# Attention scores of batches 1 to 3: one fp32 product, or two float32r products from a wider stack

## The chip, the cores and the metric

The kernel runs on one core of one Trainium2 chip. A core has a matmul engine (TensorE, PE in the rows; its weight loads are listed apart as PEld), a vector engine (VectorE, DVE), a scalar engine (ScalarE, ACT), a third elementwise engine (GpSimd, POOL) and a queue that issues the DMAs (SyncE, SP). Each engine works through its own list of instructions in order and waits for the others by semaphores. The metric is the time of one execution on the device, in microseconds (us), lower is better.

## The reference

Three stages follow one another: causal attention with a decay, and two feed-forward layers without a skip. Cut to what matters:

```python
# q, k, v: [4 batches, 8 heads, 576 tokens, 64], f: [4, 8, 576], all fp32
scores = 0.125 * q @ k^T + cum[:, None] - cum[None, :]     # cum = cumsum(log(clip(f)))
attn = softmax(causal(scores)) @ v                          # [4, 8, 576, 64] -> x: [2304, 512]
h = x @ w_in                                                # [512, 2048]
x = (h * tanh(softplus(h))) @ w_out                         # [2048, 512], weights arrive as float64
h = x @ w2_in
out = (h * cos(h)) @ w2_out                                 # [2304, 512]
```

The four weight matrices arrive in eight-byte floats and are taken apart on the chip.

## The kernel before

**Numbers in two parts.** TensorE takes fp32 operands, or float32r operands, which are fp32 words with fewer bits of the mantissa. The feed-forward products are done in float32r: a matrix is split in a high part (`h` at the end of a name) and the low rest (`l`), and three products (high by high, high by low, low by high) are added up in PSUM. The scores are done in plain fp32, in one product each.

**The stack.** For a pair of heads the attention keeps one tile `stk` with 128 rows. For the query side rows 0 to 63 hold q/8 transposed, rows 64 to 95 hold -1, row 96 holds `cum`, the rest 0. For the key side rows 0 to 63 hold k, row 64 holds `cum`, rows 96 to 127 hold 1. So one product over 128 rows gives the scaled score and the decay together. `prep_job` (L402) fills a stack: DMAs of `cum` (L410, L411), PE transposes of q and k (L429), and copies from PSUM into the stack, three of four on ACT (L445), one on DVE (L447). There are two stacks in turn (`ring`).

**Jobs and items.** A job is a pair of heads of one batch. In batch 0 a pair is cut in two jobs, (8 jobs, numbers 0 to 7); batches 1 to 3 give 12 more (8 to 19). A job of batches 1 to 3 has five items, blocks of queries, which see 64, 192, 320, 448 and 576 keys. For each item and head: `scores` (L453) issues the product (`product`, L461), DVE adds the mask and takes the maximum (L506), ACT takes the exponential (L512), POOL multiplies by the reciprocal of the sum (L526), PE transposes (L563), and PE multiplies by v (L588). An item of 576 keys is cut in two, 384 and 192 keys, since a bank of PSUM holds 512 columns.

**The filler.** From the end of the first token block of batch 0 on, PE gets other work between the attention's products: `hidden_units` (L158) computes the first layer's h for tokens that attention has finished. A unit is 12 products of 128 by 128 weights with 256, 288 or 320 tokens (`in_products`, L153); there are 128 units, and a credit spreads them over the steps of the attention. They go through the token ranges one after another. A unit needs its piece of `w_in` converted; `weight()` has this done at once if it isn't. `split_weights` (L87) does it: a DMA of 512 KB into one of three `raw` buffers, three DVE operations (L123, L124, L133), one on POOL or ACT, one on ACT (L137) and one on POOL (L138).

**The order on each engine** is that of a scheduler that reorders the written program. After the attention the rest of the units run with the conversion of `w_out`, then the two layers to the end.

Of the kernel before, what the change touches and what calls it, by code (L numbers as in the profile page):

```python
# [37 lines left out]
def tile_attention_two_ffn(  # L38
# [12 lines left out]
    nc = tc.nc  # L51
# [18 lines left out]
    rawp = ctx.enter_context(tc.tile_pool(name="raw", bufs=3))  # L70
# [8 lines left out]
    cumd = dram.tile([B * H, S], F32, name="cumd")  # L79
# [7 lines left out]
    def split_weights(layer, nm, pool, early=False):  # L87
# [18 lines left out]
        PF = 2  # L106
# [51 lines left out]
    def hidden_units(tiles, p, hbank, ready):  # L158
        for t0, T in tiles:
            while not ready(t0 + T):  # L160
                yield None
            b, at = divmod(t0, S)
            xh, xl = (xb[b][:, x, :, at : at + T] for x in range(2))
            for j in range(NJ):
                t = hbank()[:, 0:T]
                in_products(t, 1, j, xh, xl)
                if j % 2 == 0:
                    hs = p.tile([128, 2, 320], F32, tag="hs", name="hs")[:, :, 0:T]
                    nc.scalar.activation(out=hs[:, 0], in_=t, func=AF.Copy)  # L169
                else:  # L170
                    marks["v1"] = nc.vector.tensor_copy(hs[:, 1], t)
                    nc.sync.dma_start(out=hd[:, j - 1 : j + 1, t0 : t0 + T], in_=hs)
# [171 lines left out]
    def attention_units(p, bank):  # L344
# [10 lines left out]

        def span(jb):
# [45 lines left out]
        def prep_job(jb):  # L402
# [4 lines left out]
            st = ring[jb % len(ring)]  # L407
            h0 = b * H + 2 * hp
            src = cums[0][h0 : h0 + 2] if jb == 0 else cumd[h0 : h0 + 2]
            nc.sync.dma_start(out=st[96:97, :, 0], in_=src)  # L410
            nc.sync.dma_start(out=st[64:65, :, 1], in_=src)  # L411
            if jb == 0:
                marks["cum"] = nc.sync.dma_start(out=cumd, in_=cums[0])
# [12 lines left out]
            for g in groups:  # L426
# [3 lines left out]
                for which, lo in ((0, qlo), (1, 0)):  # L430
# [4 lines left out]
                    n = len(run)  # L435
                    for j in range(2):
                        i_ = t[64 * j : 64 * j + 64, at : at + n * P]
                        if jb == 0:
                            o = st[0:64, j, which, lo:khi].rearrange("r (p c) -> r c p", c=C)[:, c0 : c0 + n]
                            i_ = i_.rearrange("r (c p) -> r c p", p=P)  # L440
                        else:
                            o = st[0:64, j, which, lo + c0 * P : lo + (c0 + n) * P]
                        sc = 0.125 if which == 0 else 1.0
                        if which or j:
                            nc.scalar.activation(out=o, in_=i_, func=AF.Copy, scale=sc)  # L445
                        else:
                            nc.vector.tensor_scalar(out=o, in0=i_, scalar1=sc, scalar2=None, op0=ALU.mult)  # L447
# [5 lines left out]
        def scores(jb, i):  # L453
            st = ring[jb % len(ring)]
# [6 lines left out]
            def product(o, j, c0, c1, first=QS[i], m=r):  # L461
                at = 2 * j * S + first
# [360 lines left out]
```

## Time and profile before

| | |
|---|---|
| median of 3 runs | 1070.87 us (1069.82 to 1072.17) |
| the profiled execution | 1069.01 us, of which its span is 1067.2 us |
| PE busy | 1035.0 us, 97% of the span, 6112 instructions |
| DVE, ACT, POOL busy | 582.2, 543.3, 199.9 us |
| the score products (L463) | 384 records, 111.6 us busy (records overlap) |

A matmul's own duration in the rows holds its way through the array, so that records overlap; what a product takes from PE in a dense stretch is the distance from its start to the next one's. An fp32 product has two records. The start of a product that follows an fp32 one is shown early (28 ns after the fp32 record's start), so distances are taken to the second product behind it, less what the first takes. Times are counted from the start of the span.

### The profile page before, as it was taken

The numbers are of one execution on the slowest core, as the hardware profiler recorded it, in microseconds if no ns is written. First come the engines' busy times: TensorE is split into PE (matmuls) and PEld (weight loads), VectorE is DVE, ScalarE is ACT, GpSimd is POOL, SyncE is SP. The second block draws the span as 40 slices with busy tenths as digits, with TensorE's granted clock in tenths as the row PEclk, the third lists the DMA queues.
The fourth block names the chain that finished last, engine by engine and source line by source line (L and its number), as shares of the span: only waits on it lengthen the run. The fifth ranks groups of instructions, "written<-read, shape, count | busy, mean of one in ns | idle before, by whom it ended". The sixth has DMA issues, their size and how long they took to land. (4 is left out here: it accounts for less than half of the span.)

```text
span 1067.2 us, 17238 instructions
## 1 busy us (share of the span) xinstructions
PE 1035.0 (97%) x6112; PEld 904.2 (85%) x6112; DVE 582.2 (55%) x1390; ACT 543.3 (51%) x1168; POOL 199.9 (19%) x275
## 2 busy tenths in 40 slices
PE   5898999999999999999999999999999999999998
PEld 4577888888888889978788888899999999999997
DVE  6857544644444435756775257876445454454553
ACT  4766555655555546445656455654434343443433
POOL 6738312222111111422112002110000000000000
PEclk9999999999999999999999999999999999999999
DMA  5756422322231117765968364412010020100000
GB/s 146 179 148 167 135 73 71 91 79 79 80 83 53 57 57 238 224 201 156 326 197 310 113 200 119 143 35 89 1 60 31 1 89 1 60 31 1 30 1 29
DMA packets 119381, 111.55 MB, mean 105 GB/s; under 512 B 66672, under 2 KB 92272, under 8 KB 119296
## 3 DMA queue, kind: packets, MB, share of 16 engines
q1 hardware_dynamic: 119296, 110.46, 34.4%
q8 instruction: 48, 0.79, 0.3%
q14 instruction: 37, 0.30, 0.1%
HBM read 77.32 MB, written 33.10 MB: 103 GB/s over the span
## 5 line engine op out<-in xcount | busy, mean ns | idle before, releaser
L153 PE MATMUL h<-xb,wih 128*128 128x288 f32 (+2 forms) x848 | 190.9, 315 | 0.5 <-ACT hs L169 0.5
L153 PEld LDWEIGHTS h<-xb,wih 128*128 128x128 f32 x848 | 139.1, 190 | 11.5 <-issue 5.9
L153 PE MATMUL h<-xb,wil 128*128 128x288 f32 (+2 forms) x424 | 127.5, 302 | 0.0
L463 PE MATMUL s<-stk 128*128 128x192 f32 (+7 forms) x384 | 111.6, 419 | 9.9 <-DMA stk<-s 4.0
L526 POOL TENSOR_SCALAR s<-s,sm 128x448 f32<-128x448 f32 (+5 forms) x144 | 86.8, 616 | 166.0 <-DVE sm L524 137.2
L246 PE MATMUL acc<-wol,gh 128*128 128x512 f32 x288 | 112.7, 391 | 0.0
L246 PE MATMUL acc<-woh,gh 128*128 128x512 f32 x288 | 112.2, 390 | 0.5 <-DVE stage L268 0.5
L246 PE MATMUL acc<-woh,gl 128*128 128x512 f32 x288 | 112.2, 391 | 0.0
L512 ACT ACTIVATE s<-s,mx 128x448 f32<-128x448 f32 (+5 forms) x144 | 83.5, 581 | 52.6 <-DVE mx L506 47.6
L308 DVE TENSOR_TENSOR gl<-hl,gh 128x512 fp32r<-128x512 f32 x72 | 64.0, 890 | 67.8 <-ACT gh L303 67.7
L153 PE MATMUL hx<-x,wih 128*128 128x384 f32 x384 | 99.6, 336 | 0.0
L153 PE MATMUL h<-x,wih 128*128 128x384 f32 x384 | 97.7, 336 | 0.0
L294 ACT ACTIVATE n<-n 128x384 f32<-128x384 f32 x96 | 50.4, 525 | 91.1 <-DVE n L288 90.4
L308 DVE TENSOR_TENSOR gl<-e,gh 128x384 fp32r<-128x384 f32 x96 | 58.2, 606 | 61.3 <-ACT gh L303 61.2
L506 DVE CUSTOM_DVE_ANT_0 s<-s,maskt 128x384 f32<-128x384 f32 (+6 forms) x152 | 67.7, 453 | 37.3 <-PE s L463 30.1
L463 PEld LDWEIGHTS s<-stk 128*128 128x128 f32 (+1 forms) x384 | 64.7, 199 | 25.5 <-issue 7.1
L153 PEld LDWEIGHTS h<-xb,wil 128*128 128x128 f32 x424 | 80.4, 190 | 0.9 <-issue 0.5
L303 ACT ACTIVATE gh<-e 128x384 fp32r<-128x384 f32 x96 | 50.4, 525 | 58.6 <-DVE e L299 53.5
L138 POOL TENSOR_TENSOR wol<-raw,woh 128x512 fp32r<-128x512 f32 x32 | 44.8, 1399 | 181.3 <-ACT woh L137 176.9
L277 ACT ACTIVATE hl<-hl 128x512 f32<-128x512 f32 x72 | 45.2, 630 | 56.8 <-DMA hl<-hd 47.8
L153 PEld LDWEIGHTS hx<-x,wih 128*128 128x128 f32 x384 | 70.2, 188 | 3.8
L153 PEld LDWEIGHTS h<-x,wih 128*128 128x128 f32 x384 | 70.1, 188 | 3.7
(108 smaller groups left out, 2130.3 us busy)
## 6 DMA issues: line engine op xcount, KB each, us to landing
hl<-hd SPq DMA_DIRECT2D x72, 256.0 KB
raw<-in_moe_w_in_dram SPq DMA_DIRECT2D x32, 512.0 KB
raw<-in_moe_w_out_dram SPq DMA_DIRECT2D x32, 512.0 KB
hd<-hs SPq DMA_DIRECT2D x48, 288.0 KB
x<-yd SPq DMA_DIRECT2D x48, 192.0 KB
yd<-stage SPq DMA_DIRECT2D x32, 256.0 KB
natk<-in_k_dram SPq DMA_DIRECT2D x32, 144.0 KB
out_dram<-stage SPq DMA_DIRECT2D x18, 256.0 KB
```

The source lines that it names most:

```text
L138: nc.gpsimd.tensor_tensor(out=lo[sl], in0=f(high), in1=f(hi[sl]), op=ALU.subtract)
L153: nc.tensor.matmul(o, lhsT=a[wsl], rhs=b[:, kk, :], start=(kk == 0 and i == 0), stop=(kk == NK - 1 and i == 2),)
L246: nc.tensor.matmul(acc[ti][m], lhsT=a[:, ms], rhs=b[:, j % 2, :], start=(start and i == 0), stop=(end and i == 2),)
L277: nc.scalar.activation(out=e, in_=e, func=AF.Mish, scale=UNSCALE)
L294: nc.scalar.activation(out=t, in_=t, func=AF.Sin, scale=TWO_PI)
L303: nc.scalar.activation(out=gh, in_=e, func=AF.Copy)
L308: marks["v1"] = nc.vector.tensor_tensor(out=gl, in0=st.pop(n)[0], in1=f(gst[n][0]), op=ALU.subtract)
L463: marks["score"] = nc.tensor.matmul(o, lhsT=st.rearrange("p j w s -> p (j w s)")[0:128, at : at + m], rhs=st[0:128, j, 1, c0:c1], start=Tr ...
L506: marks["ttr"] = nc.vector.tensor_tensor_reduce(out=s[rows, c0:c1], in0=o, in1=mk, scale=-1.0, scalar=BIG if prev is None or rows.start el ...
L512: nc.scalar.activation(out=s[:, 0:w], in_=s[:, 0:w], func=AF.Exp, scale=-1.0, bias=mx, accum_out=sm[:, j : j + 1])
L526: nc.gpsimd.tensor_scalar(out=s[:, 0:w], in0=s[:, 0:w], scalar1=sm[:, j : j + 1], scalar2=1.0, op0=ALU.mult, op1=ALU.mult)
```

## The change

From batch 1 on the stack has four parts in place of two, in float32r: `[q high; q low]`, `[k high; k high]`, `[q high; -1, cum]` and `[k low; cum, 1]`, where `cum` itself is given as a high and a low row. A score product is then two products into one place of PSUM: (q high + q low) by k high, and q high by k low plus the decay. The high part is written by ACT (rounded to float32r), the low part by DVE (the source less the high part), and the second copies of the high parts by POOL. Batch 0 keeps fp32 stacks, with `cum` in two rows as well. One float32r stack is made at the start, the other takes the place of the fp32 stacks when batch 0's scores are done. The preparation of the next job begins nine half-steps before a job's end, where five were used before. Items of 576 keys are cut at 288. `hidden_units` now takes, two units at a time, a token range for which the next weights are converted, and only otherwise the least advanced one. During the attention there are two `raw` buffers and one load ahead (three and two before); the three come back behind it.

```diff
 prep_job
-            nc.sync.dma_start(out=st[96:97, :, 0], in_=src)
-            nc.sync.dma_start(out=st[64:65, :, 1], in_=src)
+            for row, x in ((96, 0), (64, 1)) if whole(jb) else ((96, 2), (64, 3)):
...
+                    for j in range(2):
+                        i_ = t[64 * j : 64 * j + 64, at : at + n * P]
+                        hi = part(slice(0, 64), which, j)
+                        nc.scalar.activation(out=hi, in_=i_, func=AF.Copy, scale=sc)
+                        nc.vector.scalar_tensor_tensor(
+                            out=part(lo_r, lo_x, j), in0=i_, scalar=sc, in1=f(hi), op0=ALU.mult, op1=ALU.subtract
+                        )
+                    both = slice(0, 2)
+                    dup = (slice(0, 64), 2) if which == 0 else (slice(64, 128), 1)
+                    nc.gpsimd.tensor_copy(part(*dup, both), f(part(slice(0, 64), which, both)))
 scores
+                for x in range(2):
+                    at = (4 * x + j) * S + first
+                    marks["score"] = nc.tensor.matmul(
+                        o, lhsT=st.rearrange("p x j s -> p (x j s)")[0:128, at : at + m],
+                        rhs=st[0:128, 2 * x + 1, j, c0:c1], start=(x == 0), stop=(x == 1),
+                    )
...
-                cuts = [(0, w)] if w <= 512 else [(0, 384), (384, w)]
+                cuts = [(0, w)] if w <= 512 else [(0, w // 2), (w // 2, w)]
 attention_units
+        def new_stack(pool, name, dt, en):
+            one = dt == F32
+            t = pool.tile([128, 2 if one else 4, 2, S], dt, name=name, bufs=1)
+            q, k = (t[:, 0], t[:, 1]) if one else (f(t[:, 2]), f(t[:, 3]))
+            nc.gpsimd.memset(q[96:128], 0.0)
+            nc.gpsimd.memset(k[64:96], 0.0)
+            en.memset(q[64:96], -1.0)
+            en.memset(k[96:128], 1.0)
+            return t
...
+        stack(late - 1)
...
-                begin = max(0, 2 * len(bl) - 5)
+                begin = max(0, 2 * len(bl) - (9 if jb + 1 < len(jobs) and not whole(jb + 1) else 5))
 hidden_units
+            have = [tl for tl in can if (1, todo[tl] // 2, "i") in converted]
+            t0, T = have[0] if have else min(can, key=todo.get)
 split_weights
-        PF = 2
+        PF = 1 if early else 2
 decay_tables
-        cums.append(cum)
+        ch, cl = (x.bitcast(F32R) for x in (ft, one))
+        nc.scalar.activation(out=ch, in_=cum, func=AF.Copy)
+        nc.vector.tensor_tensor(out=cl, in0=cum, in1=ft, op=ALU.subtract)
+        cums.extend((ft, one))
```

In the lists that follow, a row is a line of the kernel, an operation, what it writes and reads, a shape and a count. First PE, at the item of 576 keys of a late job (job 16) of the kernel before; `s` is a bank for the scores, `h` one of the filler's.

```order
L463 MATMUL s_3745<-stk_102 128x448
L463 MATMUL s_3747<-stk_102 128x448
...
L463 MATMUL s_3827<-stk_102 128x384
L463 MATMUL s_3829<-stk_102 128x384
L153 MATMUL h<-xb,wih_339 128x288 x2
L153 MATMUL h<-xb,wil_340 128x288
L153 MATMUL h<-xb,wih_339 128x288
L463 MATMUL s_3831<-stk_102 128x192 x2
```

The same place on PE with the change; `stkr` is a float32r stack, and line numbers are those of the changed kernel.

```order
L509 MATMUL s_4035<-stkr_128 128x448 x2
...
L509 MATMUL s_4038<-stkr_128 128x448 x2
...
L509 MATMUL s_4101<-stkr_128 128x288 x2
L509 MATMUL s_4104<-stkr_128 128x288 x2
L509 MATMUL s_4107<-stkr_128 128x288 x2
L509 MATMUL s_4110<-stkr_128 128x288 x2
L154 MATMUL h<-xb,wih_350 128x288 x2
```

Each fp32 product has become a pair of float32r products, and the item of 576 keys takes four banks (four names `s_`) where it took three, the two heads having shared the bank of the 192-wide part.

Second POOL, at the start of the program before: clearing of the stacks, the masks `maskt` and `mask` and then the first multiplication by a reciprocal.

```order
L607 MEMSET stk_118 32x2x576
L608 MEMSET stk_118 32x2x576
L609 MEMSET stk_118 32x2x576
L610 MEMSET stk_118 32x2x576
L666 AFFINE_SELECT maskt<-maskt 128x128
L672 AFFINE_SELECT mask_68<-mask_68 64x64 x2
L526 TENSOR_SCALAR s<-s,sm 128x128 x2
```

POOL at the same place with the change.

```order
L655 MEMSET stk_123 32x1152
L656 MEMSET stk_123 32x1152
L657 MEMSET stk_123 32x1152
L658 MEMSET stk_123 32x1152
L655 MEMSET stkr_128 32x1152
L656 MEMSET stkr_128 32x1152
L657 MEMSET stkr_128 32x1152
L658 MEMSET stkr_128 32x1152
L732 AFFINE_SELECT maskt<-maskt 128x128
L738 AFFINE_SELECT mask_68<-mask_68 64x64 x2
L572 TENSOR_SCALAR s<-s,sm 128x128 x2
```

Four more memsets, of the first float32r stack, stand ahead of the step that completes `maskt`.

Third PE at the beginning of job 8, the first job of batch 1, before: from its 64-key products to its 320-key products.

```order
L463 MATMUL s_1274<-stk_102 128x64 x2
L153 MATMUL h<-xb,wih_1171 128x256 x2
L153 MATMUL h<-xb,wil_1172 128x256
...
L463 MATMUL s_1347<-stk_102 128x192 x2
L588 MATMUL s_1283<-p,natv 64x128 x2
L153 MATMUL h<-xb,wih_1171 128x256 x4
...
L463 MATMUL s_1421<-stk_102 128x320
L463 MATMUL s_1423<-stk_102 128x320
```

The same stretch with the change.

```order
L509 MATMUL s_1301<-stkr_128 128x64 x4
L634 MATMUL s_1312<-p,natv 64x256 x8
L634 MATMUL s_1312<-p,natv 64x128 x2
L598 MATMUL s_1359<-ident,s 128x128 x3
L509 MATMUL s_1389<-stkr_128 128x192 x4
L634 MATMUL s_1402<-p,natv 64x64 x6
L449 MATMUL s_1411<-ident,natq 128x96 x5
...
L154 MATMUL h<-xb,wih_1202 128x256 x4
```

Filler has left this stretch. Counted over the whole list, 96 products (8 units) of the filler stand between the first 64-key products of jobs 8 and 9 before, and 28 (2.3 units) with the change; at the first 64-key product of job 12 both lists have some 33 units behind them, and at that of job 15 both have 51.

## Rows read from the trace of the kernel before

**Rows 1.** The profile's page: span, and busy time of PE.

```profile
span 1067.2 us, 17238 instructions
PE 1035.0 (97%) x6112; PEld 904.2 (85%) x6112; DVE 582.2 (55%) x1390; ACT 543.3 (51%) x1168; POOL 199.9 (19%) x275
```

**Rows 2.** Stretches: length, busy us of PE, PEld, DVE, ACT, POOL; clock, DMA share, GB/s.

```profile
0.00:47.40 47.40, 31.14 (x161) 21.40 (x161) 34.96 (x106) 29.22 (x81) 32.03 (x54) 0.96 0.63 161
90.00:114.00 24.00, 21.23 (x159) 17.04 (x158) 18.50 (x46) 13.71 (x37) 17.01 (x20) 0.93 0.68 179
140.00:400.00 260.00, 259.12 (x1883) 224.64 (x1882) 114.86 (x461) 136.56 (x366) 53.94 (x111) 1.00 0.26 73
```

**Rows 3.** Timeline of PE, a job of batch 2: start, us, engine, line, operation, count.

```profile
272.79 0.43 PE L153 MATMUL h<-xb,wih 128*128 128x288 f32 x2
...
273.18 1.67 PE L463 MATMUL s<-stk 128*128 128x448 f32 x4
...
274.34 0.78 PE L153 MATMUL h<-xb,wih 128*128 128x288 f32 x2
...
274.96 0.29 PE L153 MATMUL h<-xb,wil 128*128 128x288 f32 x1
```

**Rows 4.** Timeline of PE: fp32 score products of 64 and 192 keys.

```profile
285.27 0.33 PE L463 MATMUL s<-stk 128*128 128x64 f32 x2
285.41 0.51 PE L153 MATMUL h<-xb,wih 128*128 128x288 f32 x2
285.76 0.30 PE L153 MATMUL h<-xb,wil 128*128 128x288 f32 x1
...
287.97 0.82 PE L463 MATMUL s<-stk 128*128 128x192 f32 x4
288.49 0.56 PE L153 MATMUL h<-xb,wih 128*128 128x288 f32 x2
288.89 0.29 PE L153 MATMUL h<-xb,wil 128*128 128x288 f32 x1
```

**Rows 5.** Timeline of PE: float32r products of 256, 512 and 384 columns.

```profile
48.09 0.40 PE L153 MATMUL h<-xb,wih 128*128 128x256 f32 x2
...
48.45 0.40 PE L153 MATMUL h<-xb,wih 128*128 128x256 f32 x2
...
760.64 0.39 PE L246 MATMUL acc<-woh,gh 128*128 128x512 f32 x1
...
762.70 0.51 PE L153 MATMUL h<-x,wih 128*128 128x384 f32 x2
...
763.22 0.50 PE L153 MATMUL h<-x,wih 128*128 128x384 f32 x2
```

**Rows 6.** Timeline of all engines at the start; in brackets idle time and its releaser.

```profile
8.47 1.05 POOL L610 MEMSET stk<- 32x1152 f32 x1
...
9.60 0.29 POOL L666 TENSOR_SCALAR_AFFINE_SELECT maskt<-maskt 128x128 f32<-128x128 f32 x1
...
10.28 1.19 PE L463 MATMUL s<-stk 128*128 128x128 f32 x4 [4.03 <-DMA stk<-s]
...
11.62 0.29 DVE L506 CUSTOM_DVE_ANT_0 s<-s,maskt 128x128 f32<-128x128 f32 x1 [4.57 <-PE s L463]
```

**Rows 7.** Groups by shape: count, busy us, mean ns of one, idle before, its releaser.

```profile
L268 DVE SCALAR_TENSOR_TENSOR stage<-acc,stage 128x512 fp32r<-128x512 f32 x8 | 5.5, 687 | 1.8 <-ACT stage L267 1.5 <-DMA yd<-stage 0.3
...
L447 DVE TENSOR_SCALAR stk<-s 64x480 f32<-64x480 f32 x12 | 7.8, 648 | 20.9 <-PE s L429 20.9
...
L526 POOL TENSOR_SCALAR s<-s,sm 128x576 f32<-128x576 f32 x32 | 26.0, 825 | 40.4 <-DVE sm L524 40.4
```

**Rows 8.** Timeline near 22 us, DVE and POOL: a weight conversion.

```profile
20.90 0.68 DVE L133 SCALAR_TENSOR_TENSOR raw<-raw 128x512 int32<-128x512 int32 x1
...
22.36 1.29 POOL L138 TENSOR_TENSOR wil<-raw,wih 128x512 fp32r<-128x512 f32 x1
22.39 1.82 DVE L133 SCALAR_TENSOR_TENSOR raw<-raw 128x512 int32<-128x512 int32 x1
```

More of the change, by code (lines that the diff above doesn't have):

```diff
@@ L69, in tile_attention_two_ffn @@
     w0p = ctx.enter_context(tc.tile_pool(name="w0", bufs=1))
[L70 removed]
+    raw_sb = ExitStack()
+    rawp = raw_sb.enter_context(tc.tile_pool(name="raw0", bufs=2))
     ident = const.tile([128, 128], F32, name="ident")
@@ L354, in blocks, with whole @@
             return BLOCKS[1 if jobs[jb][0] // NP in CUT_BATCHES else 0]
+        def whole(jb):
+            return jobs[jb][0] // NP in CUT_BATCHES
         def span(jb):
@@ L453, in scores @@
         def scores(jb, i):
-            st = ring[jb % len(ring)]
+            st = stack(jb)
             QS, QR, _ = blocks(jb)
@@ L601, in av, with stack @@
             nc.vector.tensor_tensor(out=xl, in0=t[:, 0:width], in1=f(xh), op=ALU.subtract)
-        ring = []
-        for i in range(2):
-            ring.append(p.tile([128, 2, 2, S], F32, name=f"stk{i}", bufs=1))
-            en = nc.vector if i == 0 else nc.gpsimd
-            nc.gpsimd.memset(ring[-1][96:128, :, 0], 0.0)
-            nc.gpsimd.memset(ring[-1][64:96, :, 1], 0.0)
-            en.memset(ring[-1][64:96, :, 0], -1.0)
-            en.memset(ring[-1][96:128, :, 1], 1.0)
+        stacks, early = {}, ExitStack()
+        def new_stack(pool, name, dt, en):
[7 more added lines that the diff above has]
+            return t
+        def stack(jb):
+            key = (whole(jb), jb % 2)
+            if key not in stacks:
+                if key == (False, late % 2):
+                    early.close()
+                    pool = late_sb.enter_context(tc.tile_pool(name="stk", bufs=1))
+                else:
+                    pool = p
+                stacks[key] = new_stack(pool, f"stkr{jb % 2}", F32R, nc.gpsimd)
+            return stacks[key]
+        late = 1 + max(jb for jb in range(len(jobs)) if whole(jb)) + 1
+        e = early.enter_context(tc.tile_pool(name="stk0", bufs=1))
+        for i in range(2):
+            stacks[True, i] = new_stack(e, f"stk{i}", F32, nc.gpsimd if i else nc.vector)
             if i == 0:
                 make_masks()
+        stack(late - 1)
         for jb in range(2):
@@ L746, in tile_attention_two_ffn @@
     att_ps.close()
+    late_sb.close()
     att_sb.close()
     xsb[0].close()
+    raw_sb.close()
+    rawp = ctx.enter_context(tc.tile_pool(name="raw", bufs=3))
     attention_over = True
```

75 lines of the change are left out of this document (49 added, 26 removed).

## The prediction

> **What bounds the kernel now.** I read the page first, then the stretches, then the timeline of PE. PE is busy for 1035.0 of 1067.2 us [rows 1], more than any other engine, but a busy PE says little by itself. The stretches show where that holds: in the attention of batches 1 to 3 PE is busy for 259.12 of 260.00 us at full granted clock, while DVE, ACT and POOL have 44, 53 and 21% [rows 2]. Two stretches differ. Until 47.4 us there is no filler yet, and PE works for 31.14 us. From 90 to 114 us, where job 8 runs and the last pieces of `w_in` are converted, it loses 2.8 of 24 us, and the granted clock has a mean of 0.93, so for a while it stood at the lower of its two levels, 1.2 GHz.
>
> Second, is PE dense in the sense that one product starts when the one before lets it? Yes: three float32r products of 288 columns follow each other within 0.39 us (272.79 to 273.18), 0.131 us each [rows 3], and the timeline goes on like this over the filler. So in this stretch a microsecond taken from PE's products is a microsecond of the kernel, as long as no other engine becomes later than PE. That is the base of the forecast.
>
> **The change, part by part.** *The score products.* The pair of fp32 products of 448 columns begins at 273.18; the third filler product after it begins at 274.96, and two of 0.131 lie between, so four records took 1.52 us, 0.76 per product [rows 3], or 1.7 ns a column. The 192-wide ones: from 287.97 to 288.89, less two of 0.131, is 0.66 for two, 0.33 each; a 64-wide one: 285.27 to 285.76 less 0.26, 0.23 [rows 4]. By the price per column 320 keys cost 0.54, and 576 keys (384 and 192) 0.98. One head of one job: 0.23 + 0.33 + 0.54 + 0.76 + 0.98 = 2.84 us. With 24 heads of jobs 8 to 19 that makes 68 us.
>
> A float32r product takes 0.131 for 288 columns [rows 3], 0.12 for 256 (three in 0.36), 0.173 for 384 (three in 0.52), and 0.229 for 512 (nine from 760.64 to 762.70) [rows 5]: about 0.44 ns a column and a few ns more, so 0.145 for 320 and 0.20 for 448. Two of each: 0.29 and 0.40; the 576 keys are four of 0.131, 0.52. The 64- and 192-wide ones are the unknown term, since no float32r product of the trace is narrower than 256. Lower bound: the line through the rows goes on, 0.09 for 192 and 0.035 for 64. Upper bound: a narrow float32r product takes as long as the whole fp32 product of its width, 0.33 and 0.23. I take 0.12 for both, the narrowest one measured, because the 64-wide fp32 records show a floor: 0.115 us per record at 64 columns, where 1.7/2 ns a column would give 0.054 [rows 4]. Something other than the columns, a thing paid once per record, holds it there.
>
> So a head costs 0.24 + 0.24 + 0.29 + 0.40 + 0.52 = 1.69 us, and 24 heads 41 us. Saved: 27 us (at the lower bound 0.07 + 0.18 + 1.21 = 1.46 a head, 33 us saved; at the upper 0.46 + 0.66 + 1.21 = 2.33, 12 us saved).
>
> The page "TensorE: Matmul & The Clock Gate" of the Trainium skill has a cause for that floor: in its section "LDWEIGHTS (loading the stationary operand)" a load takes the columns over 1.2 GHz, an estimate of 0.107 us for 128 of them, whatever the product's width. Here this trace agrees with it (0.115). Its section "Back-to-back issue gap" gives 64 and 192 columns 0.029 and 0.083 instead; by that the sum would save about 33 us.
>
> *The preparation.* A job gains eight DVE operations (two each of 480, 96, 384, 192 columns), loses two, gains two on ACT and four on POOL. A DVE operation with one operand in PSUM takes 0.648 for 480 columns, 0.687 with two operands for 512 [rows 7]: the eight are some 3.6 us, less 0.9, a net 2.7 us a job. POOL's copies have 960 columns at the most; at 0.825 for 576 [rows 7] the four need 3.3 us a job. A job lasts about 24 us (260 us hold some eleven), and DVE is free for 13 of them, POOL for 19 [rows 2]. I cost this at nothing there: it begins in the first half-step of the job before and has some 20 us. If that cover were gone, the first product of each job would wait (below).
>
> *The start.* POOL gets four memsets of 1.05 us [rows 6] ahead of the step that completes `maskt`. That step ran at 9.60 and ended at 9.89; now it ends at about 14.1. DVE's first masked maximum, which stood at 11.62 and waited for PE [rows 6], then waits for POOL: +2.6 us. The split of `cum` (one more ACT and one more DVE operation of 576 columns and two more DMAs, ahead of PE's first product at 10.28) costs some 2 us as well, but beside the memsets, not after them. Until 47.4 us the chain through DVE, ACT, POOL and PE sets the pace, not PE [rows 2], so I pass the 2.6 on; lower bound 0, if the items after it close up.
>
> *Job 8.* The order takes 5.7 units of filler (12 products of 0.12, 1.4 us each, [rows 5]) out of job 8 and gives them back by job 12. PE's work doesn't change by it, but what is left in job 8 does: A late job of 24 us holds 8 units of 1.57 us (twelve times 0.131 [rows 3]), so the attention's own share of PE is some 11.5 us, with the change 9; with 2.3 units that is 12 to 13 us, and the job can't go faster than its chain. In the start stretch, without filler, items follow at some 3 us (12 in the 36 us from 11.62 to 47.4 [rows 2, 6]); five items, longer ones, need at least 16. So PE idles for 3 us or more here. Before, it lost 2.8 us in that stretch and, with the mean clock at 0.93, some 1.7 more [rows 2]. I take +2 us net, with bounds of -3 (all of that loss gone) and +8 (all 5.7 units without cover).
>
> *At nothing:* two `raw` buffers (loads wait more, which is in job 8's term), the DMAs of `cum` (fewer, each of two rows), the return of the three buffers (the order has the first loads of `w_out` some ten filler products' time ahead of the attention's end), the order of token ranges by itself.
>
> Sum: -27 + 2.6 + 2 = -22 us. Against the profiled execution's 1069.0 this gives 1046.6. The median of the runs shown is 1.9 above that execution, so 1048.5: I say 1049 us.
>
> **The rivals.**
>
> *Narrow products at fp32's price.* If float32r below 256 columns runs at the rate of fp32, only 12 us are saved: -12 + 4.6 = -7.4, 1063 us. For it: nothing so narrow was in float32r before. Against it: nothing in the rows shows such a step, and the floor explains the narrow fp32 records.
>
> *DVE and POOL get in each other's way in jobs 7 to 10.* A DVE conversion of 0.68 us took 1.82 next to a POOL operation of 1.29 that began with it [rows 8]. The change puts 16 POOL copies of about 0.8 us where conversions still run. If each delays a conversion by its length, that is 13 us of DVE time in a stretch where DVE was busy for 18.5 of 24 us [rows 2], and where units now wait for conversions; half of it would reach PE: +6, 1055 us. The page "SBUF — State Buffer" of the Trainium skill names this lock between the two engines in its opening section "Terms": whoever comes second waits for the other's whole instruction. The trace agrees (1.82 against 0.68).
>
> *The first product of a job waits for its stack, or for a bank.* This ends on the other side. The new chain is ACT, DVE and POOL in a row, and the 576-key item wants four of six banks where it had three. A wait of 1.85 us at each of twelve jobs eats the 22 us; 3 us would give 1049 + 36 = 1085. For it: PE takes its list in order, and everything behind such a product waits. Against it: a job's lead of some 20 us against about 8 us of chain, and no room for a wait of PE now (259.12 of 260 us busy [rows 2]).
>
> *No effect.* The two products take as long as the one. Rows 3 exclude it: 0.26 against more than 0.48 for 288 columns. It remains only if PE is not what the attention waits for.
>
> **The chances.** The forecast, narrow products between 0.04 and 0.15 and small losses: 0.6 (its own range 1041 to 1053). Narrow products at fp32's price 0.15; the lock in jobs 7 to 10 0.15; the waiting stack or bank 0.06; no effect 0.04. The range of 1041 to 1063 holds the first three nearly whole. What a measurement of this kernel tells from no change is about 0.2%, 2.1 us: faster 0.9, same 0.03, slower 0.07.
>
> **What would show it.** In the changed profile, distances of about 0.12 us between narrow float32r products (0.2 and more: the first rival); the attention's end some 22 us earlier than before; the first masked maximum at about 14.2 us, released by POOL; a short run of PE idle time in job 8, around 90 to 110 us; no PE idle time ahead of a job's 64-key product later on. I am wrong if PE shows idle time of 1 us or more per job after 140 us, or if the narrow distances are far from 0.12.

## The result and the profile after

The changed kernel takes 1060.6 us (median; 1057.3 to 1060.6), the kernel before beside it 1070.3 us (1069.5 to 1072.2): a ratio of 0.9896 with an interval of 0.9868 to 0.9924. One run at 1130.8 us, with TensorE's clock at 0.85, is left out as disturbed. The change is a gain of 10 us; 22 were forecast, so 1060.6 stands near the upper end of the range of 1041 to 1063. The profiled execution took 1060.6 us.

The page of the changed kernel, its span and its busy times, answers to [rows 1]:

```profile
span 1058.8 us, 17378 instructions
PE 1015.0 (96%) x6112; PEld 899.1 (85%) x6112; DVE 608.3 (57%) x1463; ACT 550.4 (52%) x1193; POOL 235.2 (22%) x331
```

PE has 20 us less to do, and the span is only 8.4 us shorter. The stretches of the changed kernel say where the rest is. The columns are those of [rows 2].

```profile
0.00:47.40 47.40, 31.99 (x160) 22.16 (x160) 30.24 (x99) 28.00 (x76) 32.28 (x53) 0.96 0.55 136
47.40:90.00 42.60, 37.80 (x270) 29.96 (x270) 27.12 (x81) 25.09 (x61) 19.51 (x28) 0.92 0.55 136
90.00:114.00 24.00, 20.20 (x168) 17.08 (x167) 17.52 (x55) 15.45 (x45) 19.36 (x27) 0.93 0.60 150
114.00:140.00 26.00, 20.78 (x154) 15.97 (x153) 21.97 (x70) 17.36 (x47) 16.34 (x23) 0.93 0.46 119
140.00:400.00 260.00, 258.27 (x2047) 238.70 (x2047) 142.19 (x526) 144.72 (x391) 81.43 (x155) 1.00 0.30 86
```

The second and the fourth stretch were left out in [rows 2]; in the kernel before they are:

```profile
47.40:90.00 42.60, 42.48 (x336) 34.50 (x336) 28.36 (x89) 27.58 (x68) 24.02 (x31) 1.00 0.55 146
114.00:140.00 26.00, 26.00 (x187) 22.64 (x186) 12.13 (x49) 13.34 (x36) 6.84 (x15) 1.00 0.38 109
```

From 140 us on PE is as dense as before (258.27 of 260 us). Between 47.4 and 90 us it loses 4.8 us where it lost 0.1, at a mean clock of 0.92 in place of 1.00. Between 90 and 140 us it loses 9.0 of 50 us where it lost 2.8, and the granted clock has a mean of 0.93 in both stretches. So the gain is there late, and something is lost early.

The late gain first. The timeline of PE shows the float32r score products of 64 and of 192 keys; these answer to [rows 4]:

```profile
287.08 0.82 PE L609 MATMUL s<-ident,s 128*128 128x128 f32 x6
287.66 0.67 PE L509 MATMUL s<-stkr 128*128 128x192 f32 x4
288.17 0.44 PE L154 MATMUL h<-xb,wih 128*128 128x288 f32 x2
...
309.02 0.61 PE L509 MATMUL s<-stkr 128*128 128x64 f32 x4
309.46 0.51 PE L154 MATMUL h<-xb,wih 128*128 128x288 f32 x2
```

Four products of 64 keys lie within 0.44 us (309.02 to 309.46), 0.11 each, and four of 192 within 0.51, 0.13 each. The forecast had 0.12 for both. The first 64-key products of two late jobs (17 and 18) stand at 309.02 and 333.02 us, 24.0 apart; before it was 311.68 and 337.95, 26.3, with 96 filler products in between in both. So a job saves 2.3 us, two heads of 1.15, the term of the prediction (2.84 - 1.69).

For the early loss one point in time is useful: the first 64-key product of **job 12**, where the lists of both kernels have the same 33 units of filler behind them. It stood at 189.6 us before and stands at 198.0 now. Four float32r jobs (8 to 11) should have brought it to 189.6 - 4 x 2.3 = 180.4. So 17.6 us are lost ahead of it, where the prediction had 4.6 (2.6 for the start, 2 for job 8). The difference of 13 us is the error of the forecast (11.6 us), within what the runs scatter. More than half of it is lost before job 8 begins: its first 64-key product has 120 filler products ahead of it in both traces and moved from 90.0 to 100.1 us. That is 10.1 us; jobs 8 to 11 lose the other 7.5. The experiments ask what these 17.6 us are.

Two pieces of the changed kernel's trace show what was followed up. The first is the start, SP's list and PE's (an SPq row is SP issuing DMAs: its start, the time of issuing, the destination and their count); it answers to [rows 6]:

```profile
7.58 2.73 SPq L425 DMA_DIRECT2D stk<-s  x4
10.37 0.86 SPq L433 DMA_DIRECT2D cumd<-s  x2
11.57 1.19 PE L502 MATMUL s<-stk 128*128 128x128 f32 x4 [5.70 <-DMA stk<-s]
13.77 0.29 POOL L732 TENSOR_SCALAR_AFFINE_SELECT maskt<-maskt 128x128 f32<-128x128 f32 x1
14.19 0.27 DVE L552 CUSTOM_DVE_ANT_0 s<-s,maskt 128x128 f32<-128x128 f32 x1
22.58 1.19 PE L502 MATMUL s<-stk 128*128 128x128 f32 x4 [1.42 <-DMA stk<-cumd]
```

The masked maximum came at 14.19 us, behind the mask, as forecast. But PE's first score product is late as well, 11.57 against 10.28, because four row DMAs are issued one after another where two were. The first filler product moved from 47.66 to 52.31 us: 4.65 us, not 2.6.

That is not the start alone. ACT's steps that write `xb`, the tokens that attention has finished, can be followed through batch 0. The first and the fourth of them, before:

```profile
28.89 0.38 ACT L600 ACTIVATE xb<-s 128x256 fp32r<-128x256 f32 x1
46.41 0.37 ACT L600 ACTIVATE xb<-s 128x256 fp32r<-128x256 f32 x1
```

and with the change:

```profile
29.22 0.38 ACT L646 ACTIVATE xb<-s 128x256 fp32r<-128x256 f32 x1
48.90 0.36 ACT L646 ACTIVATE xb<-s 128x256 fp32r<-128x256 f32 x1
```

At the first the lateness of the start had shrunk to 0.3 us, at the fourth it is 2.5. Up to 53 us DVE waits three times for loads of `w_in`, 3.0 us in all (0.5 before). The last of these waits stands right ahead of the step that releases PE for its first filler:

```profile
50.09 0.43 DVE L124 TENSOR_SCALAR raw<-raw 128x512 int32<-128x512 int32 x1 [1.44 <-DMA raw<-in_moe_w_in_dram]
51.23 0.41 DVE L647 TENSOR_TENSOR xb<-s,xb 128x256 fp32r<-128x256 f32 x1
51.78 0.88 PE L598 MATMUL s<-ident,s 128*128 128x128 f32 x3 [4.57 <-DVE xb L647]
```

The second is a load of `w_in` in job 7 of the changed kernel:

```profile
91.58 1.31 POOL L139 TENSOR_TENSOR wil<-raw,wih 128x512 fp32r<-128x512 f32 x1
93.53 0.93 SPq L105 DMA_DIRECT2D raw<-in_moe_w_in_dram  x2
98.01 0.43 DVE L124 TENSOR_SCALAR raw<-raw 128x512 int32<-128x512 int32 x1 [2.30 <-DMA raw<-in_moe_w_in_dram]
99.08 1.00 PE L609 MATMUL s<-ident,s 128*128 128x128 f32 x6 [2.05 <-DVE stkr L480]
```

POOL's subtraction is the last reader of a `raw` buffer. It ends at 92.9, the next two loads are issued at 93.5, and the conversion begins at 98.0, with DVE idle for 2.30 us ahead of it. Behind it in DVE's list stands a low part of job 8's stack (L480), and PE waits 2.05 us for that, just ahead of job 8's first product. The next piece's high half (ACT, line 138) comes only at 106.7, after one at 88.6. The last conversion of `w_in` runs at 141 us; before, it ran at 112.

Idle time has a second price. Three adjoining stretches of the changed kernel around its first filler product:

```profile
47.00:51.00 4.00, 0.21 (x4) 0.00 (x0) 2.56 (x10) 2.62 (x8) 1.25 (x5) 1.00 1.10 233
51.00:57.70 6.70, 5.92 (x20) 4.61 (x20) 3.58 (x7) 1.16 (x3) 5.70 (x6) 0.50 0.50 113
57.70:64.00 6.30, 6.30 (x59) 5.68 (x58) 4.02 (x12) 4.70 (x13) 2.70 (x4) 0.99 0.60 169
```

PE worked for 0.21 of 4 us, and then stood at the lower of its two levels (0.50, 1.2 GHz) for 6.7 us.

### The profile page after: what moved, and what is told of

Its sections match the earlier page's. It is cut to its first block, busy times and chain, and to the rows that moved or that the text cites. A ratio compares the mean times of both kernels' runs of the same rounds, so it can differ in the third digit from the quotient of the medians.

```text
span 1058.8 us, 17378 instructions
## 1 busy us (share of the span) xinstructions
PE 1015.0 (96%) x6112; PEld 899.1 (85%) x6112; DVE 608.3 (57%) x1463; ACT 550.4 (52%) x1193; POOL 235.2 (22%) x331
## 5 line engine op out<-in xcount | busy, mean ns | idle before, releaser
L154 PE MATMUL h<-xb,wih 128*128 128x288 f32 (+2 forms) x848 | 184.0, 305 | 4.1 <-ACT wih L138 3.0
L572 POOL TENSOR_SCALAR s<-s,sm 128x448 f32<-128x448 f32 (+5 forms) x144 | 82.2, 584 | 125.4 <-DVE sm L570 60.3
L552 DVE CUSTOM_DVE_ANT_0 s<-s,maskt 128x288 f32<-128x288 f32 (+6 forms) x152 | 63.6, 431 | 44.9 <-PE s L509 22.5
L248 PE MATMUL acc<-gl,woh 128*128 128x512 f32 (+1 forms) x192 | 69.2, 361 | 2.4 <-DVE gl L318 2.3
L297 DVE TENSOR_SCALAR n<-e 128x384 f32<-128x384 f32 x96 | 34.5, 359 | 64.2 <-ACT e L290 64.2
```

The costliest lines, as they stand in the source:

```text
L154: nc.tensor.matmul(o, lhsT=a[wsl], rhs=b[:, kk, :], start=(kk == 0 and i == 0), stop=(kk == NK - 1 and i == 2),)
L248: nc.tensor.matmul(acc[ti][d][:, 0:T], lhsT=a[dsl], rhs=b[:, gs], start=(start and i == 0), stop=(end and i == 2),)
L297: nc.vector.tensor_scalar(out=t, in0=e, scalar1=ROUND, scalar2=ROUND, op0=ALU.add, op1=ALU.subtract)
L552: marks["ttr"] = nc.vector.tensor_tensor_reduce(out=s[rows, c0:c1], in0=o, in1=mk, scale=-1.0, scalar=BIG if prev is None or rows.start el ...
L572: nc.gpsimd.tensor_scalar(out=s[:, 0:w], in0=s[:, 0:w], scalar1=sm[:, j : j + 1], scalar2=1.0, op0=ALU.mult, op1=ALU.mult)
```

## The experiments

Three theories stood at the beginning. **A**: the two raw buffers with one load ahead hold up the conversions, and filler comes late. **B**: the added preparation work (ACT, DVE, POOL) holds jobs 8 to 10. **C**: it is the start alone. This table holds all runs, with the ratio to the kernel before on the same chip, and three times (us) from each trace: the first filler product, and the first 64-key products of jobs 8 and 12. Unless its text says otherwise, a run is the changed kernel with the edit named. Each trace shows 395 to 406 filler products ahead of job 12, so that its time can be compared; but it is the time of one execution, and such times scatter by a microsecond (e7 changes nothing that runs ahead of its first filler product, and that stands 1.1 us later than in e2).

| run | us | ratio, interval | filler | job 8 | job 12 |
|---|---|---|---|---|---|
| before | 1070.3 | | 47.7 | 90.0 | 189.6 |
| after | 1060.6 | 0.9896, 0.9868-0.9924 | 52.3 | 100.1 | 198.0 |
| e1 before + two raw | 1076.3 | 1.0047, 1.0029-1.0066 | 51.6 | 93.9 | 196.0 |
| e2 three raw | 1057.9 | 0.9872, 0.9854-0.9890 | 50.9 | 101.4 | 196.6 |
| e3 masks first | 1059.2 | 0.9883, 0.9864-0.9902 | 53.3 | 100.0 | 197.0 |
| e4 late preparation | 1080.2 | 1.0082, 1.0063-1.0100 | 53.2 | 100.6 | 209.0 |
| e5 fp32 in batch 1 | 1065.3 | 0.9955, 0.9940-0.9971 | 53.5 | 98.6 | 203.7 |
| e6 e2 + masks first | 1057.6 | 0.9886, 0.9867-0.9905 | 50.5 | 98.7 | 193.8 |
| e7 e2 + stack by DMA | 1057.6 | 0.9883, 0.9865-0.9901 | 52.0 | 100.2 | 195.0 |
| e8 e2 + faster pace | 1060.4 | 0.9908, 0.9893-0.9922 | 55.6 | 106.4 | 195.3 |
| e9 old cuts | 1060.9 | 0.9907, 0.9890-0.9923 | 52.7 | 101.3 | 198.5 |
| e10 e2 + late memsets | 1057.3 | 0.9868, 0.9849-0.9887 | 51.6 | 99.8 | 194.6 |
| e11 e10 + old cuts | 1055.5 | 0.9859, 0.9838-0.9880 | 51.2 | 99.5 | 192.3 |
| e12 e11 + whole `cum` first | 1050.8 | 0.9823, 0.9802-0.9843 | 47.4 | 95.8 | 188.5 |

**e1: the buffers alone.** The kernel before, with this part of the change only:

```
-    rawp = ctx.enter_context(tc.tile_pool(name="raw", bufs=3))
+    rawp = raw_sb.enter_context(tc.tile_pool(name="raw0", bufs=2))
...
-        PF = 2
+        PF = 1 if early else 2
```

> The kernel before with two raw buffers and one load ahead during the attention, nothing else of the change. Theory A (the loss of about 15 us in the first 150 us comes from the two buffers: a weight conversion at the head of DVE's list waits for its DMA and everything behind it waits too): 5 to 10 us slower than before, with DVE waiting 5 us or more for raw DMAs between 20 and 150 us (2.2 before) and PE idle time there. Theory B (it comes from the added preparation work on ACT, DVE and POOL): within 2 us of before. Theory C (it is the start alone, plus what follows from it): within 2 us of before.

It is 5 us slower than before, and the interval is clear of 1. The waits of DVE from 20 to 150 us (engine and line, what it waited for; us, times, longest):

```profile
DVE raw L124 <- DMA raw<-in_moe_w_in_dram: 11.1, 7, 4.5
```

and in the kernel before:

```profile
DVE raw L123 <- DMA raw<-in_moe_w_in_dram: 2.2, 2, 1.3
```

So this part, priced at nothing, costs 5 us by itself, and 6.4 us at job 12. Its start is that of the kernel before (first masked maximum at 11.64 us), and still its first filler product comes at 51.6 us, 4.0 us late.

**e2: three buffers in the changed kernel.** One `hs` buffer less, two in place of three, makes room for the third `raw` buffer:

```
-    rawp = raw_sb.enter_context(tc.tile_pool(name="raw0", bufs=2))
+    rawp = raw_sb.enter_context(tc.tile_pool(name="raw0", bufs=3))
...
-        PF = 1 if early else 2
+        PF = 2
...
-    hsp = xsb[1].enter_context(tc.tile_pool(name="hs", bufs=3, side="right"))
+    hsp = xsb[1].enter_context(tc.tile_pool(name="hs", bufs=2, side="right"))
```

> The changed kernel with three raw buffers and two loads ahead again; for the space the filler's output tiles hs go from three to two. Theory A: 5 to 10 us faster than the changed kernel (1050 to 1055 us), DVE's wait for raw DMAs down to some 2 us. Theory B: 1058 to 1062 us, as the changed kernel; the same for theory C. If the two output tiles hurt, PE shows waits for hs after 150 us, which it doesn't in the changed kernel.

DVE's wait for `raw` fell from 6.5 us to 0.3, and yet the median fell by only 2.7 us (the intervals overlap) and job 12 came only 1.4 us earlier. The wait had moved. From 95 to 145 us PE waits longer for the converted weights themselves, 5.6 us where the changed kernel has 3.0:

```profile
PE h L154 <- ACT wih L138: 5.6, 2, 3.0
```

The two `hs` buffers do no harm: from 150 to 400 us PE shows no wait for `hs`. So A is real, but it isn't the whole loss: with the loads in time, the steps behind them are still late.

**e3: masks ahead of the new memsets.**

```
-        stack(late - 1)
+        with tc.issue_after(marks["mask"].ins):
+            stack(late - 1)
```

> The changed kernel with the four memsets of the first float32r stack held back until the masks are complete. First masked maximum at about 12.9 us in place of 14.2 (PE's first product now ends that late because of the split of cum). Theory C, or my start term: 1.3 to 2.6 us faster than the changed kernel. If the start stretch closes up behind it: no difference, within 1 us. Theories A and B say nothing of it.

The first masked maximum moved from 14.19 to 12.92 us, but the first filler product came later (53.25), and the time is that of the changed kernel within the scatter. Taken alone, this reads as "the start costs nothing". But the row DMAs and the two `raw` buffers were still there, and e12 shows that the reading is wrong.

**e4: the lead of nine half-steps taken back.**

```
-                begin = max(0, 2 * len(bl) - (9 if jb + 1 < len(jobs) and not whole(jb + 1) else 5))
+                begin = max(0, 2 * len(bl) - 5)
```

> The changed kernel with the preparation begun five half-steps before a job's end, as before the change, in place of nine. Theory B: the preparation of job 8 then collides less with the conversions, or at least differently, and the stretch of 90 to 150 us changes by some us; later, a job's first product waits for its stack, 0.5 to 2 us a job, so that the whole is 5 to 20 us slower than the changed kernel. Theory A: little change up to 150 us, and slower behind it only if the lead of nine was needed.

20 us slower than the changed kernel. Now the first products of jobs 12 and 16, the first jobs of batches 2 and 3, wait for their stack: the waits of PE from 150 to 400 us, and two stretches of the five of 50 us in it:

```profile
PE s L509 <- POOL stkr L485: 9.6, 2, 5.0
```

```profile
200.00:250.00 50.00, 44.36 (x340) 39.64 (x339) 27.10 (x100) 27.38 (x75) 16.96 (x32) 0.93 0.28 73
...
300.00:350.00 50.00, 44.60 (x338) 39.87 (x337) 26.77 (x100) 26.84 (x74) 15.37 (x31) 0.93 0.28 73
```

Two waits of nearly 5 us, and in each of the two stretches the clock's mean falls to 0.93: 2 x 50 x 0.07 = 7 us more. Not all of the 20 us lie there: job 12 is 11 us later than in the changed kernel, and its wait is 5 of them; from 115 to 140 us PE is busy for 17.8 of 25 us at a mean clock of 0.80, against 19.8 at 0.93. The two long waits are the third rival, the product that waits for its stack, made to happen; with the nine half-steps they are hidden.

**e5: fp32 scores in batch 1 too.**

```
         def whole(jb):
-            return jobs[jb][0] // NP in CUT_BATCHES
+            return jobs[jb][0] // NP < 2
```

> The changed kernel, but batch 1 keeps fp32 scores too (one product, two stack halves, the shorter lead), so that the wider preparation begins only at job 11; two raw buffers and the start as changed. Without the float32r scores of jobs 8 to 11, 4 times 2.25 us = 9 us of PE work come back (the late jobs were 24.0 us each against 26.4). Theory B (the added preparation work of jobs 8 to 10 on ACT, DVE and POOL keeps PE waiting between 90 and 150 us): the stretch from 95 to 145 us has PE busy for 46 us or more instead of 40.2, the last conversion of w_in ends near 120 us instead of 141, and the time is 1056 to 1062, no slower than the changed kernel. Rival (the loss is the late start and the two raw buffers, whatever the scores): the stretch stays as in the changed kernel, the last conversion ends after 130 us, and the time is 1067 to 1071.

1065.3 us: between the two. So are the signs: from 95 to 145 us PE is busy for 44.5 us (46 or more was asked for B), and the last conversion runs at 131.8 us. The run is 4.7 us slower than the changed kernel (4 x 2.3 = 9.2 were given up), and 5.7 us later at job 12. So some 3.5 us of batch 1's saving are lost with its float32r jobs themselves, by their preparation or because PE isn't what those jobs wait for; this run doesn't part the two. By this one trace B holds for a fifth of the 17.6 us, not for most. In e1 job 12 stood at 196.0 with the same fp32 scores, so what e5 has beside the two buffers (the start, the cuts, the float32r stacks' memsets) costs 7.7 us there.

**e6, e7: masks first, and the second stack, on e2.** e6 joins the edits of e2 and e3. e7 takes the constant rows of the stack that is made in job 8 from the first one:

```
+            if not one and len(stacks) == 3:
+                o = stacks[False, (late - 1) % 2]
+                nc.sync.dma_start(out=q[64:128], in_=f(o[64:128, 2]))
+                nc.sync.dma_start(out=k[64:128], in_=f(o[64:128, 3]))
+                return t
             nc.gpsimd.memset(q[96:128], 0.0)
```

> The two small gains of before together: three raw buffers with two loads ahead (with two hs buffers for the space), and the float32r stack's memsets behind the masks. Each alone gave -2.8 and -1.4 us against the changed kernel. If the start and the loads are separate causes: 1056.0 to 1056.8. If both act only through the time of the first conversions: 1057.5 to 1058, as with three buffers alone, and the first filler product stays at 51 us or later.

> Three raw buffers, and the second float32r stack, which is made in job 8 by four POOL memsets (4.5 us, from 96.8 to 101.4 in the run with three buffers), takes its constant rows from the first stack by two DMAs. If those memsets, ahead of a conversion step in POOL's list, are what makes filler late in job 8: conversions 11 to 16 come 3 to 4 us earlier, PE's waits for wih (5.6 us from 95 to 145) fall under 3 us, and the time is 1054 to 1055.5. If POOL has slack there: 1057 to 1058.5.

Neither can be told from e2. POOL's four memsets of job 8 looked like the cause (4.5 us right ahead of a conversion step), and taking them out alone gains nothing. As with e3, that doesn't show that they are free where another delay lies beside them.

**e8: conversions at a faster pace, on e2.**

```
-        elif val % 4 == 1:
+        elif val % 3 == 1:
```

> Three raw buffers, and a piece of w_in is converted at every third half-step instead of every fourth while the attention of batches 0 and 1 runs; by the order, 6 units of filler stand between the first 64-key products of jobs 8 and 9 instead of 3, and 13 instead of 10 ahead of job 8. Supply theory (from job 8 on PE lacks filler because w_in is converted too late, and the attention's chain alone can't fill it): PE's lost time from 75 to 150 us falls from some 17 us to 8 or less, no half-clock stretch after 100 us, the time is 1048 to 1053. Theory B (the added preparation work itself holds the items): the loss stays above 13 us wherever the units stand, 1055 to 1058. If conversions pushed into batch 0 take its chain's time on DVE: the first filler and job 8 come later and the time is 1058 or more.

This gives job 8 its filler back (six units, from three), and the run is slower than e2, which it is built on; the intervals don't touch. The third reading is what came: the conversions take their place in batch 0's chain, the first filler product comes at 55.6, job 8 at 106.4, and the clock has a mean of 0.66 from 25 to 50 us:

```profile
25.00:50.00 25.00, 20.01 (x93) 13.05 (x92) 20.41 (x57) 16.69 (x47) 16.74 (x23) 0.66 0.59 143
100.00:125.00 25.00, 19.92 (x139) 15.01 (x138) 18.96 (x56) 16.02 (x43) 20.25 (x25) 0.86 0.34 87
```

In 100 to 125, where the units now stand, PE is still busy for only 19.9 of 25 us. But over the whole stretch that the supply theory spoke of it did gain. First e2, then e8:

```profile
75.00:150.00 75.00, 67.04 (x493) 54.98 (x492) 54.83 (x160) 45.66 (x119) 46.92 (x64) 0.91 0.50 134
75.00:150.00 75.00, 69.92 (x532) 59.65 (x529) 50.26 (x156) 45.96 (x120) 42.11 (x59) 0.95 0.48 132
```

Idle time and clock together cost 8.0 + 75 x 0.09 = 14.7 us in e2 and 5.1 + 75 x 0.05 = 8.8 us in e8, close to the 8 that the theory asked for. The gain is lost again in the start and behind 150 us (PE is busy for 46.6 us from 150 to 200). So the run doesn't refute the supply theory: the supply is a part of the loss, and this edit buys it at too high a price.

**e9 to e11: the cut of the 576 keys, and the first stack's memsets.** e9 undoes one line of the change. Two cuts of 288 take a bank per product, four in all; with 384 and 192 the narrow halves of both heads share one.

```
-                cuts = [(0, w)] if w <= 512 else [(0, w // 2), (w // 2, w)]
+                cuts = [(0, w)] if w <= 512 else [(0, 384), (384, w)]
```

> The changed kernel, but the 576 keys are cut at 384 again instead of 288: the 192-wide halves of both heads share a bank, so the item takes three banks instead of four. PE's work grows by 24 times 0.036 us = 0.9 us (0.173 + 0.111 against two of 0.133, twice). By the order, 4.3 units of filler stand between the first 64-key products of jobs 8 and 9 instead of 2.3. If the fourth bank is what holds the items and pushes filler back from 0 to 150 us (a part of the change that was priced only as a rival): PE's lost time there falls from 55 to 48 us or less and the time is 1052 to 1056. If banks have nothing to do with it: 1060 to 1062.

e10 adds to e2 that the float32r stack's memsets are issued in job 5, and e11 is e10 with the old cuts:

```
+            if jb == late - 3:
+                with tc.issue_after(marks["nrm"].ins):
+                    fills.pop()()
...
-            nc.gpsimd.memset(q[96:128], 0.0)
-            nc.gpsimd.memset(k[64:96], 0.0)
-            en.memset(q[64:96], -1.0)
-            en.memset(k[96:128], 1.0)
+            def fill():
...
+            if one or len(stacks) > 2:
+                fill()
+            else:
+                fills.append(fill)
```

> Three raw buffers, and the four POOL memsets of the first float32r stack come in job 5 instead of ahead of the masks, so that POOL's start is as before the change. If the memsets are the start's whole cost: first masked maximum at 11.5 to 12.5 us, first filler product at 48 to 49 us instead of 51, and 1053.5 to 1056 against 1057.9 with three buffers alone. If the shift is made up anyway, or comes from the split of cum: first filler at 50 us or later, 1057 to 1058.5.

> The run with late memsets, and the 576 keys cut at 384 again. By the order, 7.7 units of filler stand between the first 64-key products of jobs 8 and 9, as in the kernel before (8). If filler in job 8 with the bank is the main loss: PE busy for 46 us or more from 95 to 145 us (40.2 in the changed kernel), 1046 to 1051. If the added preparation work itself is: no better than with late memsets alone by more than 1 us.

e9 alone changes nothing. e10 alone changes little, and its start shows why:

```profile
7.59 2.74 SPq L428 DMA_DIRECT2D stk<-s  x4
11.59 1.19 PE L505 MATMUL s<-stk 128*128 128x128 f32 x4 [6.03 <-DMA stk<-s]
12.93 0.29 DVE L555 CUSTOM_DVE_ANT_0 s<-s,maskt 128x128 f32<-128x128 f32 x1 [4.88 <-PE s L505]
```

POOL is out of the way now, and the masked maximum waits for PE, which waits for the row DMAs: 12.93 where 11.62 was before. e11 has the best time so far and job 12 at 192.3, but its interval overlaps that of e10, so the gain of the cuts with enough buffers (1.8 us) is not shown. From 95 to 145 us PE is busy for 43.4 us, where 46 was the sign for filler and bank as the main loss (40.2 in the changed kernel).

**e12: job 0 takes its decay row whole.**

```
-                    for y in range(2):
-                        nc.sync.dma_start(out=st[row + y : row + y + 1, x], in_=cums[y][h0 : h0 + 2])
+                    nc.sync.dma_start(out=st[row : row + 1, x], in_=cums[2][h0 : h0 + 2])
...
-        cums.extend((ft, one))
+        cums.extend((ft, one, cum))
```

> The run with three buffers, late memsets and the old cuts, and job 0 takes its decay row whole in fp32 (row 96, row 64), as the kernel before did, with the second row left at zero: two DMAs of two rows instead of four, and none of them behind the split of cum, which now feeds only the DRAM copy for the jobs from 1 on. If the split and its DMAs were what is left of the start (first score product at 11.57 us instead of 10.28, first masked maximum at 12.92 instead of 11.62 with the memsets out of the way): first score product at 10.3 to 10.6, first masked maximum at 11.6 to 12, job 8 one to two us earlier than 99.5 us, and 1053 to 1055 against 1055.5. If the shift is made up before the first filler product: that one stays at 51 us and the time at 1055 to 1056.

1050.8 us, the fastest of all: 20.2 us under the kernel before on its chip (1071.0), and by the ratios 8 us under the changed one, with intervals that don't touch. That is more than was expected (1053 to 1055). The interval of e11 is just touched, so there the trace has to decide. The start of e12:

```profile
7.59 1.47 SPq L427 DMA_DIRECT2D stk<-s  x2
10.29 1.19 PE L504 MATMUL s<-stk 128*128 128x128 f32 x4 [4.26 <-DMA stk<-s]
11.64 0.29 DVE L554 CUSTOM_DVE_ANT_0 s<-s,maskt 128x128 f32<-128x128 f32 x1 [3.59 <-PE s L504]
```

Every row is back where [rows 6] had it, and the first filler product stands at 47.4 us, 3.9 us earlier than in e11 and 3.1 us earlier than in any other run with three buffers; job 12 comes 3.8 us earlier than in e11. A delay of 1.3 us at 10 us went with one of almost 4 at 50. It was not the wait alone that changed: the scheduler's lists differ too (the second step of the first conversion, on DVE, stands ahead of the fourth item's masked maxima in e12 and behind them in e11), and no run parts the two. What stays lost is in the stretches of e12:

```profile
90.00:114.00 24.00, 16.73 (x126) 13.81 (x126) 19.89 (x47) 11.62 (x30) 19.63 (x22) 0.86 0.49 131
114.00:140.00 26.00, 24.69 (x188) 21.94 (x188) 16.51 (x59) 15.73 (x45) 10.87 (x19) 1.00 0.44 133
140.00:400.00 260.00, 258.87 (x2056) 238.55 (x2055) 148.40 (x539) 153.44 (x410) 81.90 (x155) 1.00 0.31 88
```

The second is nearly full again (24.69 of 26 us, against 20.78). In 90 to 114, job 8 with its conversions, PE is idle for 7.3 us. Most of that is one wait, for the eleventh converted piece of `w_in`, just ahead of job 8's first product:

```profile
94.00 0.69 ACT L138 ACTIVATE wih<-raw 128x512 fp32r<-128x512 f32 x1 [0.83 <-DVE raw L134]
94.75 1.23 PE L154 MATMUL h<-xb,wih 128*128 128x256 f32 x4 [4.44 <-ACT wih L138]
```

The tenth piece comes at the time of the kernel before (81.51 against 81.39 us), the eleventh 5.5 us later; before it was

```profile
88.50 0.70 ACT L137 ACTIVATE wih<-raw 128x512 fp32r<-128x512 f32 x1 [1.59 <-DVE raw L133]
```

In e12 POOL has finished its step of that piece at 87.75 us, and DVE's last step begins only at 93.29. In between DVE works through five low parts of job 8's stack (L482, from 87.72 to 91.28), masked maxima and the first step of the next conversion. That is theory B seen in the rows; no run takes it away.

## Why the prediction came out as it did

The time lies in the stated range, and that is partly luck. The forecast's own range ended at 1053 us; the rest, up to 1063, was put in for two rivals, narrow products at fp32's price and the lock between DVE and POOL, and the runs show neither. The saving was right, and the losses were too low: 4.6 us where the traces have 17.6 at job 12. So the attention ended some 9 us earlier (its last products with v begin at 394.0 us, against 403.4), not 22.

- **The score products, -27 us: right.** 0.11 and 0.13 us for the narrow products against 0.12, and 2.3 us per late job against 2.3. The first rival (narrow products at fp32's price, 0.33 and 0.23) is refuted, though its time of 1063 is near what was measured: a time alone wouldn't have parted them. The page "TensorE: Matmul & The Clock Gate" of the Trainium skill gives for the load of 128 columns, in its section "LDWEIGHTS (loading the stationary operand)", 0.107 us as an estimate; this trace agrees with it for float32r too (0.11 at 64 columns). The 0.029 that the prediction worked out from the formula in the page's section "Back-to-back issue gap" doesn't come out here; the section itself says of this formula that it under-counts narrow products.
- **The start, +2.6 us: the first rows right, the size wrong, and one part misplaced.** The masked maximum came at 14.19 us, released by POOL, as said. The step that failed is "the split of `cum` ... beside the memsets, not after them". Two delays that lie beside each other at the first masked maximum are not one delay: PE's first product and the rows behind it are late by the DMAs whether POOL is late or not. So undoing the memsets gave nothing that can be told (e3, e10), and undoing the DMAs behind that gave 3.9 us by the ratios and 4.7 by the medians (e12 against e11). A third delay lies beside them: at the first filler product the two buffers alone cost 4.0 us (e1), the start with three buffers 3.2 us (e2), and both together 4.65 us. The clock at 1.2 GHz for 6.7 us came on top.
- **Two raw buffers, at nothing: wrong.** e1 puts 5 us on them in the kernel before. In the changed kernel giving them back is worth some 2.7 us (the intervals overlap), and the wait goes on to the next step of the conversion.
- **Job 8, +2 us with bounds of -3 and +8: too low, and in the wrong place.** The prediction looked for the idle time in job 8. Job 8's first product is already 10.1 us late, and the loss goes on to 140 us, because the conversions end at 141 and not 112. PE loses 9.0 us between 90 and 140 us where it lost 2.8, and the mean clock of 0.93 takes another 50 x 0.07 = 3.5 us, against 1.7. The reason given, filler taken out of job 8, is a part of it: e8 put the filler back and won 6 us between 75 and 150, at the price of the start. The working also took a late job as 24 us; it takes 26.3, so that its attention had 13.7 us of PE and not 11.5, and the same sum would have left PE idle for half of the 3 us it found.
- **The preparation, at nothing: right for the stack, wrong for the conversions.** With the lead of nine half-steps no late job waits for its stack. But the low parts stand in DVE's list between the steps of a conversion while job 7 runs, and PE then waits for the converted weights: 4.4 us at one place in e12.
- **The rivals.** The lock between DVE and POOL isn't seen to have grown: the last step of a conversion took 816 ns on the mean of 20 to 150 us, against 895 before, and the step ahead of it 841 against 846. The product that waits for its stack doesn't come after 140 us; e4 shows its price when the lead is short. That the two products take as long as the one is excluded by the 2.3 us per late job.

By job 12 the ledger of 17.6 us reads, from the runs in their order: 1.4 for the buffers (e2), 2.0 for the memsets (e10), 2.3 for the cuts (e11) and 3.8 for the `cum` rows (e12), 9.5 in all; each holds behind the edits ahead of it, not alone, and the first three are little above the scatter of single traces. 8.1 us stay. 5.8 of them are there at job 8's first product (95.8 us against 90.0), with the wait of 4.4 us for the eleventh piece. e5 gives the float32r jobs of batch 1 some 3.5 us. Whether what stays is the added work on DVE and POOL or that a chain without filler gains nothing from shorter products, no run here parts.

The rule for the filler's token ranges, by the weights that are converted, was priced at nothing; no run here tests it.

## What to carry to other kernels

A saving on the busiest engine is worth its price only where that engine is what ends last; sum it by stages, and price the warm-up, where a chain sets the pace, by its rows' starts. When two delays lie beside each other, undoing either shows nothing: undo both before calling one free. Work that is hidden where it is needed can still stand in another engine's list ahead of work that is not: read the lists, not only the waits. A buffer taken away "for space" is a term of the sum: look up who reads it last, and how long a load takes from there.

## What the runs showed of the hardware that wasn't expected

Between 64 and 288 columns the price of a float32r product moves only from 0.11 to 0.13 us: the narrow products of a head, 4 of its 12, cost nearly what the 288-wide ones do. A wait of PE is paid twice where it is followed by the lower clock: 4 us almost idle and then 6.7 us at 1.2 GHz (half the full clock, so some 3.4 us lost) in the changed kernel, 9.6 us of waits and some 7 us of clock in e4.
